# Fixed slots per expert, ranks counted during the attention, and a large-score path at the end: hashed attention with a cosine router on one core

## The chip, the cores and the metric

One core of a Trainium2 chip runs the whole program. The metric is the device time of one execution in microseconds. TensorE (PE) runs matmuls and loads their weights (PEld), VectorE (DVE) and ScalarE (ACT) do elementwise work, GpSimd (POOL) does some elementwise work and issues indirect DMAs, and SyncE (SP) issues the other DMAs. All numbers are 32-bit floats unless bf16 is named.

## The reference, cut to what matters

Attention runs over 4 batches, 8 heads, 768 positions and 64 dimensions. Each query and key gets a bucket from 6 sign bits (its product with `proj`), and a query attends only to keys of its own bucket. The 3072 rows of 512 numbers then go to one of 8 experts each.

```python
q_bits = (np.einsum('bhsd,dk->bhsk', q, proj) > 0)
mask = q_bucket[:, :, :, None] == k_bucket[:, :, None, :]
scores = np.where(mask, scale * np.matmul(q, k.transpose(0, 1, 3, 2)), -1e9)
attn = softmax(scores)
x = (attn @ v).transpose(0, 2, 1, 3).reshape(3072, 512)
logits = normalised(x) @ normalised(expert_emb).T / tau
expert_idx = np.argmax(logits, axis=1)
gate_w = softmax(logits)[np.arange(N), expert_idx]
for e in range(8):
    m = expert_idx == e
    out[m] = gate_w[m, None] * (np.maximum(x[m] @ w1[e], 0) @ w2[e])
```

`w1[e]` is 512 x 1024 and `w2[e]` is 1024 x 512, 2 MB each.

## The kernel before, in words

**Attention.** Work goes by 16 pairs of heads (four per batch). A pair has 12 units (two halves of the queries, six chunks of 128 keys), taken three at a time in four groups. For a group, `scores` makes the products of q and k and of their bucket bits on PE and the exponentials on ACT (L285), and DVE adds them up (L289, L292); `attend` (L300) multiplies the exponentials of the group before with v. Beside the groups stand the steps of the neighbouring pairs. In group 0 these are `prep_features` of q of the next pair (L250 transposes, L251 copies; L246 squares q and k on ACT, for the test of large scores, ahead of the copy) and `sums` (L314) of the pair before. In group 1 they are the same for k, and `finish` (L330, L334, DVE L337 to L348) of the pair before. In group 2 they are `prep_bits` (L263, with DVE L265 for `qb` and L268 for `kb`) and the loads on SP three pairs ahead. The PSUM tiles called `banks` are three buffers of two banks, handed around. `prep_experts` (L195, called at L364) normalises the expert embedding: a load on SP (L197), a square on ACT (L202), a root on POOL, `en` on DVE (L210) and four transposes on PE (L214). It is called before the first scores.

**Routing.** After the last pair of a batch, `route` takes the squares of x on ACT (L133), the best expert and its gate on DVE and POOL, writes the one-hot choice to `oh_all`, and stores the batch with its gates to `xd` in DRAM from SP (L161).

**Between the stages.** If any score could be large, `attention_any` would do the attention again. Every engine reads `beyond_i` and jumps over it (L476). Then PE counts all tokens (L486, L488), DVE makes from this the slot of each token (L490 to L540), 24 small products on PE turn these into a list of token numbers (L546), and `src` (L549) holds it. An expert's tokens fill whole tiles of 128, so 31 tiles always suffice, and 31 are run.

**Experts.** For each tile, `fetch` reads the tile's expert number on SP, loads that expert's `w1` and `w2` (L565, L567, two buffers) and gathers 128 rows from `xd` on POOL (L569). `turn_x` transposes them (L579, copied by L581). The first product has 64 matmuls of 128 columns (L593; a float32 product is two instructions), with a relu on ACT after each half (L596). The second product has 16 matmuls of 512 columns (L601). DVE multiplies by the gate (L603) and POOL scatters the rows (L604). Numbers past the last token are dropped.

The code is issued to each engine in an order that the framework chooses close to the order of the text; each engine then runs its own list in order.

Of the kernel before, what the change touches and what calls it, by code (L numbers as in the profile page):

```python
# [10 lines left out]
U32 = mybir.dt.uint32  # L11
ACT = mybir.ActivationFunctionType
# [3 lines left out]
P = 128  # L16
# [9 lines left out]
def kernel(  # L26
# [26 lines left out]
    NT = (N + E * (P - 1)) // P  # L53
# [31 lines left out]
    iota_t = iota("iota_t", [P, NT], [[1, NT]])  # L85
    iota_n = iota("iota_n", [P, NBLK], [[P, NBLK]])

    tok = iota("tok", [P, B, NC], [[S, B], [1, NC]], base=-N, cm=NC)
# [17 lines left out]
    xh = tc.dram_tile([B * H, S, D], F32, name="xh")  # L106
    half = const.tile([P, NC], F32, name="half")
    nc.vector.memset(half[:], 0.5)
    seg = const.tile([P, E, NBLK], F32, name="seg")
# [12 lines left out]
    oh_all = const.tile([P, E, NBLK], F32, name="oh_all")  # L122
# [3 lines left out]
    BF16 = mybir.dt.bfloat16  # L126


    def route(b, x, l, rp):
        ss = rp.tile([P, NC], F32, name="ss", tag="ss")  # L130
        for c in range(NC):
            sq = rp.tile([P, DM], F32, name="sq", tag="sq")
            nc.scalar.activation(sq[:], x[:, c, 0:DM], ACT.Square, accum_out=ss[:, c : c + 1])  # L133
# [9 lines left out]
        idx = rp.tile([P, NC], F32, name="idx", tag="idx")  # L143
        nc.vector.tensor_reduce(out=idx[:], in_=cand[:], axis=AX.X, op=ALU.min)
        nc.vector.tensor_tensor(
            out=oh_all[:, :, b * NC : (b + 1) * NC].rearrange("p e c -> p c e"),
            in0=iota_e[:].unsqueeze(1).broadcast_to([P, NC, E]),
            in1=idx[:].unsqueeze(2).broadcast_to([P, NC, E]), op=ALU.is_equal,
# [12 lines left out]
        nc.sync.dma_start(xd[b * S : (b + 1) * S, :].rearrange("(p c) w -> p c w", c=NC), x[:])  # L161

# [4 lines left out]
    with ExitStack() as at:  # L167
# [55 lines left out]
        ld, feat, acc, av, zs, xb, lgh = {}, {}, {}, {}, {}, {}, {}  # L223

# [13 lines left out]
        def prep_features(pr, i):  # L238
# [5 lines left out]
            if i == 0:  # L244
                sq = rp.tile([P, 4 * NC * D], F32, name="qksq", tag="qksq", bufs=1)
                nc.scalar.activation(sq[:], qk[:].rearrange("p i c h d -> p (i c h d)"), ACT.Square,  # L246
                                     accum_out=squares[:, pr : pr + 1])
# [3 lines left out]
            nc.scalar.activation(t[:], ps[:, :, 0:SH], ACT.Copy, scale=1.0 if i else DOWN)  # L251

# [69 lines left out]
        def finish(pr):  # L322
# [4 lines left out]
            z, W = zs.pop(pr), P + 2 * E  # L327
            zt = banks()
# [3 lines left out]
            for s in range(2):  # L332
                for c in range(HC):
                    nc.tensor.matmul(ps[:, s, c * W : (c + 1) * W], lhsT=av[pr, s][:, c * P : (c + 1) * P],  # L334
                                     rhs=iden[:, j, :], start=True, stop=True)
            rz = small.tile([P, HC, 4], F32, name="rz", tag="rz")
# [27 lines left out]
        prep_experts()  # L364
        U, PU = len(units), 2 * NC
        for u0 in range(0, U + PU, G):
# [6 lines left out]
            pr, g = u0 // PU, u0 % PU // G  # L373
            if g == 0:
# [3 lines left out]
            elif g == 1:  # L378
                prep_features(pr + 1, 1)
                if pr > 0:  # L380
                    finish(pr - 1)
            elif g == 2:
                prep_bits(pr + 1)
                load(pr + 3)

# [89 lines left out]

    with tc.If(nc.values_load(beyond_i[0:1, 0:1], min_val=0, max_val=1) > 0):  # L476
        attention_any()


    with ExitStack() as so:  # L480
        sp = pool("sp", 1, so)
        ps_o = pool("ps_o", 1, so, space=PSUM)
        flat = "p e n -> p (e n)"

        cnt = ps_o.tile([P, E, NBLK], F32, name="cnt")
        nc.tensor.matmul(cnt[:].rearrange(flat), lhsT=ones[:], rhs=oh_all[:].rearrange(flat), start=True, stop=True)  # L486
        rank = ps_o.tile([P, E, NBLK], F32, name="rank")
        nc.tensor.matmul(rank[:].rearrange(flat), lhsT=tri[:], rhs=oh_all[:].rearrange(flat), start=True, stop=True)  # L488
        upto = sp.tile([P, E, NBLK], F32, name="upto")
        nc.vector.tensor_tensor_scan(out=upto[:].rearrange(flat), data0=seg[:].rearrange(flat),  # L490
                                     data1=cnt[:].rearrange(flat), initial=0.0, op0=ALU.mult, op1=ALU.add)

        full = sp.tile([P, E, NBLK], F32, name="full")
        nc.vector.tensor_tensor(out=full[:], in0=upto[:, :, NBLK - 1 : NBLK].broadcast_to([P, E, NBLK]),  # L494
                                in1=iota_n[:].unsqueeze(1).broadcast_to([P, E, NBLK]), op=ALU.is_gt)
        tiles = sp.tile([P, E], F32, name="tiles")
        nc.vector.reduce_sum(out=tiles[:], in_=full[:], axis=AX.X)
        tend = sp.tile([P, E], F32, name="tend")
        nc.vector.tensor_tensor_scan(out=tend[:], data0=ones[:, 0:E], data1=tiles[:], initial=0.0,
                                     op0=ALU.mult, op1=ALU.add)  # L500

        past = sp.tile([P, NT, E - 1], F32, name="past")
        nc.vector.tensor_tensor(out=past[:], in0=iota_t[:].unsqueeze(2).broadcast_to([P, NT, E - 1]),  # L503
                                in1=tend[:, 0 : E - 1].unsqueeze(1).broadcast_to([P, NT, E - 1]), op=ALU.is_ge)
        texp = sp.tile([P, NT], F32, name="texp")
# [54 lines left out]
    def fetch(t):  # L560
        if t >= NT:
            return
# [74 lines left out]
```

## Time and profile before

| | us |
|---|---|
| median of 3 runs (lowest to highest) | 948.99 (948.25 to 949.33) |
| the profiled execution | 949.78 |
| span of its profile, first to last instruction | 948.1 |
| PE busy | 873.2 (92%) |
| DVE busy | 320.5 (34%) |
| ACT busy | 265.1 (28%) |
| POOL busy | 72.8 (8%) |

The mean granted clock of TensorE is 0.967 of 2.4 GHz. A row of the order of time gives start, duration, engine, line, operation, output and inputs, how many instructions it merges, and in brackets the idle time of the engine before it with what ended it. Matmuls are pipelined: the recorded duration of one is longer than the distance to the next, so distances of starts are the better measure.

### The profile page before, as it was taken

What the parts mean: (1) busy time and instruction counts of PE and PEld (TensorE: products, weight loads), DVE (VectorE), ACT (ScalarE), POOL (GpSimd) and SP (SyncE); (2) the same over time, 40 slices, a digit from 0 to 9 for tenths busy, and PEclk for the clock granted to TensorE, in tenths of its full rate; (3) what the DMA queues carried; (4) which work ended last, traced back from release to release, by engine and by line L of the source; (5) the groups of instructions that cost most, each with busy time, mean ns of one, the idle gap of its engine ahead of it and who ended that gap; (6) DMA issues with size and microseconds to landing.
All of it is one profiled execution on the core that took longest, in us unless ns stands there. A gap on an engine that the chain in (4) does not pass through costs nothing.

```text
span 948.1 us, 12969 instructions
## 1 busy us (share of the span) xinstructions
PE 873.2 (92%) x5397; PEld 538.3 (57%) x5397; DVE 320.5 (34%) x521; ACT 265.1 (28%) x389; POOL 72.8 (8%) x85
## 2 busy tenths in 40 slices
PE   2999999999999999990699999999999999999996
PEld 1444444444444444440576766767677676766764
DVE  4656666666666676655000010101001010000100
ACT  3555555555655554431000100001010000101000
POOL 2000000000000000000101110101111010110100
PEclk8999999999999999995599999999999999999998
DMA  8122223211222210001498889888888888889850
GB/s 196 38 52 50 50 51 118 51 45 39 102 50 50 51 68 1 1 1 69 183 392 307 314 312 325 305 320 313 306 312 313 313 321 312 314 309 323 302 215 1
DMA packets 109121, 170.56 MB, mean 180 GB/s; under 512 B 53302, under 2 KB 57398, under 8 KB 108545
## 3 DMA queue, kind: packets, MB, share of 16 engines
q1 hardware_dynamic: 104064, 155.23, 48.6%
q0 software_dynamic: 4992, 14.44, 3.9%
q8 instruction: 44, 0.72, 0.3%
q14 instruction: 21, 0.16, 0.1%
HBM read 157.06 MB, written 14.43 MB: 181 GB/s over the span
## 4 chain that ended last, share of the span: by engine, by line
issue 27%; DMA 24%; PE 1%; DVE 1%; POOL 0%; POOLq 0%; DVEq 0%
DMA out_dram<-y,src 24%; PE slot L546 1%; DVE row L535 0%; POOL xg L569 0%; POOLq L632 0%; DVE col L538 0%; DVE col L540 0%; DVE pos L521 0%; POOLq L604 0%; DVE upto L490 0%; POOLq L569 0%; DVE past L503 0%; DVE pos_e L519 0%; DVE full L494 0%; DVE pos_e L516 0%
## 5 line engine op out<-in xcount | busy, mean ns | idle before, releaser
L593 PEld LDWEIGHTS ps_h<-xgt,w1t 128*128 128x128 f32 x1984 | 230.1, 193 | 32.4 <-ACT ht L596 18.1
L593 PE MATMUL ps_h<-xgt,w1t 128*128 128x128 f32 x1984 | 236.1, 277 | 10.8 <-ACT ht L596 10.8
L601 PE MATMUL ps_y<-w2t,ht 128*128 128x512 f32 x496 | 218.0, 592 | 0.0
L285 ACT ACTIVATE p<-banks 128x768 f32<-128x768 f32 x192 | 153.5, 810 | 98.0 <-PE banks L282 94.1
L279 PE MATMUL banks<-qt,kt 64*128 64x384 f32 x768 | 165.9, 510 | 3.9 <-ACT p L285 2.4
L596 ACT ACTIVATE ht<-ps_h 128x512 f32<-128x512 f32 x62 | 37.0, 597 | 464.3 <-PE ps_h L593 464.3
L601 PEld LDWEIGHTS ps_y<-w2t,ht 128*128 128x128 f32 x496 | 91.9, 190 | 103.8 <-issue 103.8
L292 DVE TENSOR_TENSOR acc<-acc,p 128x768 f32<-128x768 f32 x128 | 122.7, 958 | 73.9 <-ACT p L285 64.1
L300 PE MATMUL av<-p,vt 128*64 128x385 f32 x768 | 138.1, 495 | 0.0
L603 DVE TENSOR_SCALAR y<-ps_y,xg 128x512 f32<-128x512 f32 x31 | 23.2, 750 | 323.8 <-PE ps_y L601 323.8
L279 PEld LDWEIGHTS banks<-qt,kt 64*128 64x128 f32 x768 | 64.7, 188 | 69.2 <-issue 37.5
L300 PEld LDWEIGHTS av<-p,vt 128*64 128x64 f32 x768 | 49.5, 136 | 76.5 <-issue 76.5
L282 PE MATMUL banks<-qb,kb 64*128 64x384 bf16 x384 | 63.6, 325 | 0.0
L604 POOL DMA_INDIRECT out_dram<-y,src x31 | 31.5, 1015 | 409.4 <-DVE y L603 409.4
L581 DVE COPY xgt<-ps_x 128x512 f32<-128x512 f32 x31 | 21.5, 693 | 111.4 <-PE ps_x L579 101.0
L289 DVE TENSOR_TENSOR acc<-p,p 128x768 f32<-128x768 f32 x32 | 30.6, 957 | 29.9 <-ACT p L285 29.6
L250 PE MATMUL banks<-ident,qk 128*128 128x128 f32 x192 | 29.3, 291 | 8.2 <-DMA qk<-in_q_dram 7.9
L250 PEld LDWEIGHTS banks<-ident,qk 128*128 128x128 f32 x192 | 21.5, 146 | 26.6 <-issue 25.9
L151 POOL TENSOR_TENSOR nrm<-ss,half 128x6 f32<-128x6 f32 x4 | 5.3, 1335 | 403.9 <-ACT sq L133 403.9
L282 PEld LDWEIGHTS <-kb 64*128 64x128 bf16 x384 | 19.5, 95 | 25.3 <-issue 0.9
L569 POOL DMA_INDIRECT xg<-xd,src x31 | 30.3, 977 | 39.4 <-DVE src L549 30.3
L268 DVE TENSOR_SCALAR kb<-banks,ksub 32x768 bf16<-32x768 f32 x32 | 32.5, 1017 | 0.5
(125 smaller groups left out, 395.4 us busy)
## 6 DMA issues: line engine op xcount, KB each, us to landing
w1t<-in_moe_w_dram SPq DMA_DIRECT2D x31, 2048.0 KB, 9.3
w2t<-in_moe_w_dram SPq DMA_DIRECT2D x31, 2048.0 KB, 10.3
xd<-xb SPq DMA_DIRECT2D x4, 1539.0 KB, 6.4
qk<-in_q_dram SPq DMA_DIRECT2D x32, 192.0 KB, 3.8
qk<-in_k_dram SPq DMA_DIRECT2D x32, 192.0 KB, 3.7
vt<-in_v_dram SPq DMA_DIRECT2D x16, 384.0 KB, 3.1
xg<-xd,src POOLq DMA_INDIRECT x31, 7.5
out_dram<-y,src POOLq DMA_INDIRECT x31, 7.6
```

The source lines that it names most:

```text
L250: nc.tensor.transpose(ps[:, c // HC, (c % HC) * P : (c % HC + 1) * P], qk[:, i, c, :, :], ident[:])
L268: nc.vector.tensor_scalar(out=kb[h * D : h * D + 32], in0=ps[h * D + 32 : h * D + 64, :, 0:SH], scalar1=0.0, scalar2=ksub[h * D + 32 : h * ...
L279: nc.tensor.matmul(ps[:, h, 0:SH], lhsT=kt[rows[h], c // HC, kc], rhs=qt[rows[h], s, :], start=True, stop=False)
L282: nc.tensor.matmul(ps[:, h, 0:SH], lhsT=kb[rows[h], c // HC, kc], rhs=qb[rows[h], s, :], start=False, stop=True)
L285: nc.scalar.activation(p[:, :, 0:SH], ps[:, :, 0:SH], ACT.Exp, scale=ESCALE)
L289: nc.vector.tensor_tensor(out=a[:], in0=pts[(u - 1) % NPT][:, :, 0:SH], in1=p[:, :, 0:SH], op=ALU.add)
L292: nc.vector.tensor_tensor(out=a[:], in0=a[:], in1=p[:, :, 0:SH], op=ALU.add)
L300: nc.tensor.matmul(ps[h * D : (h + 1) * D, 0 : SH + 1], lhsT=vt[:, h, c, :], rhs=p[:, h, 0 : SH + 1], start=(c == 0), stop=(c == NC - 1))
L593: nc.tensor.matmul(ps[:, f, :], lhsT=a[:, d, f * P : (f + 1) * P], rhs=xt[:, d, :], start=(d == 0), stop=(d == ND - 1))
L596: nc.scalar.activation(ht[:, f - 3 : f + 1, :], ps[:, f - 3 : f + 1, :], ACT.Relu)
L601: nc.tensor.matmul(py[:], lhsT=ht[:, f, :], rhs=b[:, f, :], start=(f == 0), stop=(f == NF - 1))
L604: nc.gpsimd.indirect_dma_start(out=out[:, :], out_offset=bass.IndirectOffsetOnAxis(ap=src[:, t : t + 1], axis=0), in_=y[:], in_offset=None ...
```

## The change

- **Slots.** Each expert gets three fixed tiles of 128 slots (384 tokens). What is past 384 goes to guarded tiles, of which 25 are written out in nested tests. A tile is run only if the number `nt` of such tiles, worked out on the chip, says so.
- **Ranks per batch.** `count`, `place` and `fill` do the counting, placing and listing for one batch, for batches 0 to 2 inside the attention of the next batch (`count` in `finish` of its pair 0, `place` as a generator from which each group takes four steps, `fill` in `finish` of its pair 1). Batch 3 is placed behind the first expert product. Masks and token numbers are bf16, the numbers in two parts.
- **Early tiles.** Experts 0 and 1 keep their first 256 slots for batches 0 to 2. These four tiles are gathered in the next to last pair and turned before the last `finish`. Their products stand directly behind the attention, and the third tiles of the two experts follow as late tiles.
- **Experts.** A first product takes all tiles of an expert at once (256, 384 or 128 columns), with a relu per 128 hidden rows in one of four PSUM banks. Weights are loaded once per expert, and once per guarded tile that needs others.
- **Large scores.** The jump over `attention_any` is at the end of the program, with an expert stage of its own behind it.
- **Order.** `prep_experts` is called in the fourth group of the first pair. The square of q and k comes behind the copy of k. POOL writes zeros to the last batch's rows of `xd` at the start.

```diff
-    NT = (N + E * (P - 1)) // P
+    KT, EARLY = 3, 2
+    NS = E * KT
+    NO = (N - EARLY * P + EARLY * (2 * P - 2)) // P
...
+    def count(b, cnt, rank):
+        nc.tensor.matmul(cnt, lhsT=ones_b[:], rhs=oh_all[:, b].rearrange("p e c -> p (e c)"), start=True, stop=True)
+        nc.tensor.matmul(rank, lhsT=tri_b[:], rhs=oh_all[:, b].rearrange("p e c -> p (e c)"), start=True, stop=True)
...
+        if b == B - 2:
+            nc.vector.tensor_tensor(out=base[:], in0=upto[:, :, NC - 1], in1=least[:], op=ALU.max)
...
+        yield nc.vector.tensor_tensor(out=rows[:, b], in0=iota_p[:].unsqueeze(1).broadcast_to([P, NC, P]),
+                                      in1=row[:].unsqueeze(2).broadcast_to([P, NC, P]), op=ALU.is_equal)
...
+    def fill(b, ps):
+        col = cols.pop(b)
+        for c in range(NC):
+            nc.tensor.matmul(ps, lhsT=rows[:, b, c], rhs=col[:, c].rearrange("p i t -> p (i t)"),
+                             start=(c == 0), stop=(c == NC - 1))
+        nc.vector.tensor_tensor(out=slots[:], in0=slots[:], in1=ps[:, 0:NS], op=ALU.add)
+        nc.vector.tensor_tensor(out=slots[:], in0=slots[:], in1=ps[:, NS : 2 * NS], op=ALU.add)
...
+    nc.gpsimd.memset(xgs[0][:], 0.0)
+    nc.gpsimd.dma_start(xd[(B - 1) * S : N, :].rearrange("(p c) w -> p c w", c=NC),
+                        xgs[0][:].unsqueeze(1).broadcast_to([P, NC, XW]))
...
-            if i == 0:
-                sq = rp.tile([P, 4 * NC * D], F32, name="qksq", tag="qksq", bufs=1)
...
             nc.scalar.activation(t[:], ps[:, :, 0:SH], ACT.Copy, scale=1.0 if i else DOWN)
+            if i == 1:
+                sq = rp.tile([P, 4 * NC * D], BF16, name="qksq", tag="qksq", bufs=1)
...
-        prep_experts()
...
+            run(4)
...
+            elif g == 3 and pr == 0:
+                prep_experts()
             elif g == 2:
                 prep_bits(pr + 1)
                 load(pr + 3)
+                if pr == 2 * NP:
+                    bring1(0, 0)
+                    bring2(0, 0)
+                if pr == len(pairs) - 2:
+                    early = [[gather(src[0][:, e * KT + i : e * KT + i + 1]) for i in range(2)] for e in range(EARLY)]
+        for e in range(EARLY):
+            ps = banks()
+            for i in range(2):
+                turn_x(xgt[e], i, early[e][i][0], ps[:, i, :])
+        finish(len(pairs) - 1)
...
-    with tc.If(nc.values_load(beyond_i[0:1, 0:1], min_val=0, max_val=1) > 0):
...
+        ps_x, ps_h, ps_y = turns(2, "ps_x"), turns(4, "ps_h"), turns(2, "ps_y")
...
+        def hidden(i, xt, n):
+            for f in range(NF):
+                ph = ps_h()
+                for d in range(ND):
+                    nc.tensor.matmul(ph[:, 0:n], lhsT=w1s[i][:, d, f * P : (f + 1) * P], rhs=xt[:, d, 0:n],
+                                     start=(d == 0), stop=(d == ND - 1))
+                nc.scalar.activation(ht[:, f, 0:n], ph[:, 0:n], ACT.Relu)
...
+        hidden(0, xgt[0], 2 * P)
+        ps = ps_x()
+        count(B - 1, ps[:, 0 : E * NC], ps[:, E * NC : 2 * E * NC])
+        for _ in place(B - 1, ps[:, 0 : 2 * E * NC].rearrange("p (t n) -> p t n", t=2), sp):
+            pass
+        result(0, early[0])
+        fill(B - 1, ps_x()[:, 0 : 2 * NS])
+        late = [tiles_of(e, 2) for e in range(EARLY)]
+        hidden(1, xgt[1], 2 * P)
+        turn(0, late[0])
+        result(1, early[1])
+        nxt = tiles_of(EARLY, 0)
+        hidden(0, xgt[0], P)
...
+        for e in range(EARLY, E):
...
+            hidden(i, xgt[i], KT * P)
...
+            turn(1 - i, nxt)
+            result(i, tiles)
...
+        nt = nc.values_load(ctl[0:1, 2 * NO : 2 * NO + 1], min_val=0, max_val=NO)
+        with ExitStack() as rest:
+            for t in range(NO):
+                rest.enter_context(tc.If(nt > t))
...
+                hidden(i, xgt[i], P)
...
+    with tc.If(nc.values_load(beyond_i[0:1, 0:1], min_val=0, max_val=1) > 0, preferred_fallthrough_block=False):
         attention_any()
...
+        experts_any()
```

## Rows read from the trace of the kernel before

**Rows 1.** Busy time of each engine by stretches, with granted clock and DMA share

```profile
core 0: us, PE busy (x) PEld busy (x) DVE busy (x) ACT busy (x) POOL busy (x), PEclk, DMA share, GB/s
0.00:23.80 23.80, 5.82 (x33) 3.63 (x33) 10.03 (x38) 8.13 (x11) 5.70 (x19) 0.88 0.89 197
23.80:422.20 398.40, 393.11 (x2690) 188.87 (x2693) 250.43 (x375) 215.40 (x302) 4.02 (x3) 0.99 0.18 49
...
433.00:472.80 39.80, 15.09 (x65) 13.81 (x66) 11.35 (x26) 0.00 (x0) 2.96 (x3) 0.50 0.36 137
472.80:939.90 467.10, 456.25 (x2593) 330.14 (x2592) 42.60 (x59) 37.02 (x62) 57.80 (x58) 1.00 0.84 302
939.90:948.10 8.20, 0.07 (x1) 0.00 (x0) 0.75 (x1) 0.00 (x0) 0.98 (x1) 0.70 0.00 0
```

**Rows 2.** Order of time, the start

```profile
9.63 1.28 ACT L246 ACT_TABLE_LOAD   x1 [9.63 <-DMA qk<-in_k_dram]
10.92 1.48 ACT L246 ACTIVATE qksq<-qk 128x1536 f32<-128x1536 f32 x1
...
16.24 0.41 SPq L197 DMA_DIRECT2D emb<-in_moe_expert_emb_dram  x1
...
16.66 2.05 DVE L268 TENSOR_SCALAR kb<-banks,ksub 32x768 bf16<-32x768 f32 x2
...
20.84 0.63 ACT L202 ACTIVATE emb_sq<-emb 8x512 f32<-8x512 f32 x1 [0.27 <-DMA emb<-in_moe_expert_emb_dram]
...
23.30 0.56 PE L214 MATMUL banks<-ident,en 8*128 8x8 f32 x4 [7.77 <-DVE en L210]
...
23.80 1.65 PE L279 MATMUL banks<-qt,kt 64*128 64x384 f32 x4
```

**Rows 3.** Order of time on PE, an expert tile, and the last second product

```profile
497.21 7.03 PE L601 MATMUL ps_y<-w2t,ht 128*128 128x512 f32 x16
...
504.08 3.73 PE L593 MATMUL ps_h<-xgt,w1t 128*128 128x128 f32 x32
...
507.65 0.60 PE L579 MATMUL ps_x<-ident,xg 128*128 128x128 f32 x4
...
508.56 3.84 PE L593 MATMUL ps_h<-xgt,w1t 128*128 128x128 f32 x32 [0.31 <-ACT ht L596]
...
932.94 7.03 PE L601 MATMUL ps_y<-w2t,ht 128*128 128x512 f32 x16
```

**Rows 4.** DMA issues: how many, size, median us from issue to landing

```profile
w2t<-in_moe_w_dram SPq DMA_DIRECT2D x31, 2048.0 KB, 10.3
xd<-xb SPq DMA_DIRECT2D x4, 1539.0 KB, 6.4
...
xg<-xd,src POOLq DMA_INDIRECT x31, 7.5
```

**Rows 5.** Order of time, from the last routing to the first expert product

```profile
433.12 0.34 SPq L161 DMA_DIRECT2D xd<-xb  x1
...
440.13 0.55 DVE L490 TENSOR_TENSOR_SCAN upto<-seg,cnt 128x192 f32<-128x192 f32 x1 [7.04 <-SPq L476]
...
445.82 3.35 DVE L535 TENSOR_TENSOR row<-iota_p,rf 128x3072 f32<-128x3072 f32 x1
...
450.22 10.42 PE L546 MATMUL slot<-col,row 128*128 128x31 f32 x48 [14.32 <-DVE col L540]
...
472.78 5.05 PE L593 MATMUL ps_h<-xgt,w1t 128*128 128x128 f32 x32
```

**Rows 6.** Waits in the attention (us, times, longest), then the end of it in time

```profile
PEld banks L279 <- DVE kb L268: 7.7, 12, 1.1
...
PEld banks L279 <- ACT qksq L246: 5.6, 9, 0.6
...
423.96 1.64 PE L334 MATMUL banks<-iden,o 128*128 128x144 f32 x12
...
426.69 0.23 DVE L348 TENSOR_TENSOR lgh<-banks,rz 128x48 f32<-128x48 f32 x1
```

**Rows 7.** PE's sequencer at the jump, L476: duration min/median/max in ns, start

```profile
L476 PEldq COMPARE_BRANCH  x1: 3532/3532/3532, 428.5 to 428.5; - x1
```

More of the change, by code (lines that the diff above doesn't have):

```diff
@@ L161, in route @@
         nc.sync.dma_start(xd[b * S : (b + 1) * S, :].rearrange("(p c) w -> p c w", c=NC), x[:])
+    base = const.tile([P, E], F32, name="base")
+    nc.vector.memset(base[:], 0.0)
+    least = const.tile([P, E], F32, name="least")
+    nc.vector.memset(least[:], 0.0)
+    nc.vector.memset(least[:, 0:EARLY], 2.0 * P)
+    rows = const.tile([P, B, NC, P], BF16, name="rows")
+    tile_all = const.tile([P, B, NC], F32, name="tile_all")
+    slots = const.tile([P, NS], F32, name="slots")
+    nc.vector.memset(slots[:], 0.0)
@@ new lines, with bring1, bring2 @@
+    NW = 2
+    w1s = [const.tile([P, ND, F], F32, name="w1_0")]
+    w2s = [const.tile([P, NF, DM], F32, name="w2_0")]
+    NX = 6
+    xgs = [const.tile([P, XW], F32, name=f"xg{i}") for i in range(NX)]
+    xgt = [const.tile([P, ND, KT * P], F32, name=f"xgt{i}") for i in range(2)]
+    def bring1(i, e, **kw):
+        nc.sync.dma_start(w1s[i][:], w1[bass.ds(e, 1)].rearrange("o (c p) f -> p (o c) f", p=P), **kw)
+    def bring2(i, e, **kw):
+        nc.sync.dma_start(w2s[i][:], w2[bass.ds(e, 1)].rearrange("o (c p) m -> p (o c) m", p=P), **kw)
@@ L223, with run @@
         ld, feat, acc, av, zs, xb, lgh = {}, {}, {}, {}, {}, {}, {}
+        steps = []
+        def run(n):
+            for _ in range(n):
+                if steps and next(steps[0], None) is None:
+                    steps.pop(0)
         def load(pr):
@@ L327, in finish @@
             z, W = zs.pop(pr), P + 2 * E
+            if j == 1 and b > 0:
+                run(99)
             zt = banks()
@@ L335, in finish @@
                                      rhs=iden[:, j, :], start=True, stop=True)
+            if j == 0 and b > 0:
+                count(b - 1, ps[:, 0, HC * W : HC * W + E * NC], ps[:, 1, HC * W : HC * W + E * NC])
+                steps.append(place(b - 1, ps[:, :, HC * W : HC * W + E * NC], rp))
+                next(steps[0])
+            elif j == 1 and b > 0:
+                fill(b - 1, zt[:, 1, 0 : 2 * NS])
             rz = small.tile([P, HC, 4], F32, name="rz", tag="rz")
@@ L363 @@
         prep_bits(0)
-        prep_experts()
         U, PU = len(units), 2 * NC
-        for u0 in range(0, U + PU, G):
+        early = []
+        for u0 in range(0, U + G, G):
             for u in range(u0, u0 + G):
@@ L573, in turn_x @@
-    def turn_x(t):
-        if t >= NT:
-            return
-        a, b, x = got[t]
-        ps = ps_x.tile([P, DM], F32, name="ps_x", tag="ps_x")
-        for d in range(ND):
-            nc.tensor.transpose(ps[:, d * P : (d + 1) * P], x[:, d * P : (d + 1) * P], ident[:])
-        xt = hp.tile([P, ND, P], F32, name="xgt", tag="xgt")
-        nc.vector.tensor_copy(out=xt[:], in_=ps[:].rearrange("p (d n) -> p d n", n=P))
-        got[t] = a, b, x, xt
-    fetch(0)
-    fetch(1)
-    turn_x(0)
```

365 lines of the change are left out of this document (251 added, 114 removed).

## The prediction

> **What bounds the kernel now.** I read the split of the span into stages first [rows 1]. The attention stretch (23.8 to 422.2) has PE busy for 393 of 398 us at a granted clock of 0.99, with DVE busy for 250 (63%) and ACT for 215. The expert stretch (472.8 to 939.9) has PE busy for 456 of 467 us at 1.00 (2.4 GHz), with the DMA engines at 0.84. Both are PE's, so only PE time removed there counts. Three stretches are not PE's: the start, where the first score matmul stands at 23.80 [rows 2]; the routing gap from 433 to 472.8, with PE busy for 15 of 40 us at 0.50 (1.2 GHz); and a tail of 8.2 us. Then I read the steady expert tile [rows 3]: 16 matmuls of 512 columns start at 497.21 and what follows them at 504.08, so they take 6.87 (0.429 each); half a first product, 32 matmuls of 128 columns, goes from 504.08 to 507.65, 3.57 (0.112 each), and there are two halves; transposes (0.60) and a wait for ACT (0.31) are the rest. From 497.21 to the last second product at 932.94 there are 29 steps of 15.03 us. The program runs 31 tiles because the bound on the number of padded tiles is 31.
>
> **How many tiles there will be.** The inputs have a fixed seed. The reference's own routing gives 464, 461, 375, 317, 367, 377, 373 and 338 tokens. With three fixed tiles per expert that is 24 tiles, and experts 0 and 1 overflow by one each: 26 tiles, five fewer. The first three batches put 337 and 328 tokens on experts 0 and 1, so the 256 early slots are full and cost no extra tile.
>
> **Start.** In the trace the first scores stand behind the four transposes of `prep_experts`, which wait for `en`, which waits for a small load that SP issues only at 16.24 [rows 2]. That is moved behind the third group of the first pair. What is then last is `kb`, done at 16.66 + 2.05 = 18.71. The square of q and k (1.48 + 0.19) no longer stands ahead of the first copy on ACT: 17.0. Against this stands a new transfer: zeros into the last batch's rows of `xd`, 768 rows from POOL, about the 1539 KB whose store takes 6.4 us [rows 4], while the DMA engines are at 0.89 [rows 1]. It can cost nothing or at most the 4.6 us from its issue near 5 to the landing of k at 9.63; the loads of pair 0 were mostly issued before it, so I take 1.3. Scores then start at 18.3, a gain of 5.5 (2.2 to 6.8). On POOL, the memsets of `qb` and `kb` come behind the new memset and this issue; POOL is busy for 5.70 us in this stretch [rows 1] and `kb` is written at 16.66, so several us cover them.
> The Trainium skill (DMA: Bandwidth & Descriptors, section Queues, rings and completion order) says that each DMA engine takes turns between the queues that have work, a packet at a time. By that the loads would run at half speed while the zeros go, the start would gain 2.2 and the sum come out 3.3 us higher; no row of this trace shows both queues busy there.
>
> **Attention.** Three times, PE gets 2 counting and 6 slot matmuls in bf16. The nearest row is L546: 48 instructions of 31 columns in 10.42 us at the lower clock [rows 5], so 0.217 each, about 0.11 at the upper level: 24 x 0.11 = 2.6 us. They have a single pass where the row's have two; none is free on a full PE, so 1.3 to 5.2. `prep_experts` costs its 0.56 of transposes here and a wait of 0 to 2.5 (its chain from 20.84 to 23.30 [rows 2]): I take 1.0 in all, because ACT and DVE have idle time ahead of it. Moving the square behind the copy of k gives back part of the 5.6 us for which weight loads wait on it, mostly on ACT standing at a load [rows 6]: 2.5 (0 to 5.6). Placing a batch is about 22 DVE instructions, mostly on a quarter of the elements of L490's 0.55 us [rows 5], one row test a quarter as wide as L535 (0.84), and the adds of the slots: about 6 us per batch, spread four steps to a group. A pair takes 24.9 us, of which DVE uses 15.7, so the idle 9 hide it; without that cover it would be 18 us in all. SP gets 4 MB of weights at the ninth pair, when DMA is at 0.18 [rows 1]; POOL gets four gathers that wait for the slots of batches 0 to 2, with 25 us before their use. Sum: +1.1.
>
> **From attention to the first expert product.** The last matmuls of `finish` (L334) end at 425.60 [rows 6]. Ahead of them stand 4 x 4 transposes, 0.60 each four [rows 3]: 2.4. The PSUM banks are read until 426.92 by L348, so another 1.0 (0 to 1.3). The first expert product starts at 429.0 - 5.5 + 1.1 = 424.6, in place of 472.78 [rows 5]. What was between is hidden: the routing of batch 3 (425.6 to 433.1), its store, the jump, the placing (440.1 to 460.6), the gather and the first weights. On ACT the relus come behind the squares and an exponential of this routing; four `ps_h` banks hold the first 4 x 1.7 us of products, which is just enough.
>
> **Expert stage.** The rows give 0.112 at 128 columns and 0.429 at 512; a straight line gives 0.217 at 256 and 0.323 at 384, and three pieces of 128 would bound the last from above at 0.335 (+5 us in all). First product: six experts x 64 x 0.323 = 124, two early ones of 256 columns 27.8, two late and two overflow tiles 4 x 7.14 = 28.6. Second product: 26 x 6.87 = 178.6. Transposes: 22 tiles x 0.60 = 13.2, and 0.5 at each of six turns of three tiles, which have two banks: 3. Last count and slots 0.9. Sum 376.1, or 14.5 us per tile. Weights fall from 31 to 10 loads of 4 MB; each has 20 us or more of cover where it now lands in 10 [rows 4].
> The late tiles' chain: store of `xd` issued at 433.1 + 2.4 - 4.4 = 431, landed by 438; slots ready behind the second product of expert 0, at 424.6 + 13.9 + 13.7 + 1 = 453; gather 1.1 + 7.5 [rows 4], and two scatters ahead on POOL at 1.3: 464, needed at 467. It holds by 3 us.
>
> **Branches and tail.** The jump over the large-score code goes from its present place to the end, and the two overflow tiles stand in nested tests. One jump is in the trace: PE's compare took 3.53 us [rows 7]. PE's two taken bodies follow the test directly, and queued matmuls cover them, so I take 1.0 for both (0 to 7.1). The exits cost PE nothing that anyone waits for; at the very end SP has to pass two exits after the last scatter: 1.5 (0 to 4). The tail is otherwise the same 8.2.
> The Trainium skill (Runtime: NRT & Kernel Launch, section Instruction fetch mechanics) states that a taken branch to code outside the fetched window stalls for a fetch, which speaks against putting tests into the expert stage; PE's 3.53 us agrees, and by it alone at each of three tests the sum would be 9.6 higher, the second rival below.
>
> **Sum.** 424.6 + 376.1 + 1.0 + 8.2 + 1.5 = 811.3 of span. The profiled execution is 949.78 for a span of 948.1, so 1.7 lies around it: 813.0. The median shown, 948.99, is 0.8 lower: 812.2.
>
> **Rivals.**
> 1. DVE doesn't hide the placing: PE waits for 18 us over three batches: 830. For it: DVE feeds `kb` and the accumulators, and weight loads already wait 7.7 us on `kb` [rows 6]. Against: 9 us idle in each pair. Chance 0.13.
> 2. Every test costs PE the 3.53: two bodies and the last exit, with the 1.0 replaced: 822. For: [rows 7]. Against: in that row PE had nothing queued. Chance 0.12.
> 3. The late tiles come 5 to 10 us late, because the slack of 3 us is used up by POOL or the store: 820, a little more with the clock. Chance 0.09.
> 4. The early tiles don't do what they are for: the first product waits until the store of `xd` lands (439.5 now), through a buffer taken over from the attention. PE idles for 14 us and restarts at 1.2 GHz for some 5 us of work, as the 5.07 against 3.57 of the first half tile shows [rows 3, 5]: 830. Chance 0.07.
> 5. Slower than before: the expert stage runs at 1.2 GHz. Each us of its work then costs one more; the 137 us gained are gone once 137 of the 376 do so, and all of it gives 1188. For: the clock was at 0.50 over the gap. Against: over 467 us it was 1.00 with a wait such as the 0.31 us in every tile [rows 1, 3], and the new order has fewer. Chance 0.02.
>
> **How the numbers follow.** The sum has 0.56. I predict 812.2. The low ends of start (-1.3), attention (-4), banks (-1), turns (-3) and tests with tail (-2.5) give 801; rivals 1 to 4 reach 830, and with the upper ends of the start (3.3) and of the straight line (4.6) 838. 801 to 838 leaves out rival 5 and mixes. About 0.2% is what a measurement of this kernel can tell from no change; only rival 5 and things unseen lie there: faster 0.97, same 0.01, slower 0.02.
>
> **What the new profile would show.** First score matmul near 18; the square behind the copy of k; the attention's last L334 near 424 and first expert product near 425; clock 1.00 throughout; 384-column matmuls 0.32 us apart; 26 scatters; PE's last product near 802. Wrong if PE idles over 3 us anywhere behind the attention, if pairs 5, 9 and 13 (counted from 0) are longer than others, or if more than two guarded tiles run.

## The result, and the profile after

The changed kernel takes 824.65 us (median of four runs, 823.36 to 826.12) against 949.16 (948.25 to 950.64) for the kernel before: ratio 0.8687, 95% interval 0.8669 to 0.8706. 812.2 was predicted, with a range of 801 to 838. The profiled execution took 824.79 for a span of 822.7, where the sum had 811.3: the sum is 11.4 short. Every part below is counted in spans.

Busy time by stretches, the same view as [rows 1] (clock, DMA share and GB/s at the end of a line):

```profile
core 0: us, PE busy (x) PEld busy (x) DVE busy (x) ACT busy (x) POOL busy (x), PEclk, DMA share, GB/s
0.00:23.80 23.80, 4.20 (x19) 3.02 (x23) 7.99 (x41) 4.64 (x6) 6.67 (x21) 1.00 0.97 172
23.80:422.00 398.20, 388.84 (x2684) 186.47 (x2678) 262.85 (x448) 215.52 (x305) 8.64 (x8) 1.00 0.25 67
422.00:450.00 28.00, 26.56 (x155) 19.16 (x152) 12.18 (x35) 9.34 (x25) 1.34 (x1) 1.00 0.53 207
...
500.00:800.00 300.00, 297.78 (x994) 165.00 (x993) 29.62 (x44) 29.13 (x68) 37.60 (x38) 0.99 0.41 144
800.00:822.70 22.70, 9.97 (x44) 5.79 (x43) 1.44 (x2) 1.11 (x4) 1.00 (x1) 0.81 0.09 23
```

The gap of [rows 1], 40 us at 0.50 with PE busy for 15, is gone: from 422 to 450 PE is busy for 26.56 of 28 at 1.00. DMA's share in the expert stretch is 0.41, where it was 0.84. But the first 23.8 us have PE busy for 4.20 (5.82 before), and DVE's busy time in the attention rose by 12.4.

The start, in order of time, to be read beside [rows 2]:

```profile
4.27 0.95 POOL L270 DMA_DIRECT2D xd<-xg  x1
...
8.99 8.30 SPq L363 DMA_DIRECT2D qk<-in_k_dram  x1
...
17.95 2.79 PE L376 MATMUL banks<-ident,qk 128*128 128x128 f32 x12 [17.95 <-DMA qk<-in_q_dram]
...
20.06 1.48 ACT L380 ACTIVATE qksq<-qk 128x1536 bf16<-128x1536 f32 x1
...
21.55 0.79 ACT L377 ACTIVATE qt<-banks 128x768 f32<-128x768 f32 x1
...
29.38 2.22 ACT L415 ACTIVATE p<-banks 128x768 f32<-128x768 f32 x3 [4.39 <-PE banks L412]
```

POOL issues the zeros at 4.27. SP then stands for 8.30 us at one load of k, and the first transposes wait for q until 17.95; they stood at 7.90 before. The first exponential is at 29.38 (before: 25.81). It was to come 5.5 earlier and comes 3.6 later. The square still runs ahead of the copy of q: the order of the text was changed, but not the order in which the framework issued it, and this holds for every pair (below).

PE, in order of time, from the attention's last value product to the end (x is a count; the second column runs to the end of the group):

```profile
425.33 4.10 PE L430 MATMUL av<-p,vt 128*64 128x385 f32 x24
...
435.83 14.08 PE L692 MATMUL ps_h<-xgt,w 128*128 128x256 f32 x64 [1.42 <-DVE beyond L543]
...
521.62 20.80 PE L692 MATMUL ps_h<-xgt,w 128*128 128x384 f32 x64
542.26 1.04 PE L284 MATMUL ps_x<-ident,xg 128*128 128x128 f32 x8
...
776.77 7.31 PE L692 MATMUL ps_h<-xgt,w 128*128 128x128 f32 x64
786.30 0.90 PE L284 MATMUL ps_x<-ident,xg 128*128 128x128 f32 x4 [2.22 <-DMA xg<-xd,osrc]
787.00 8.52 PE L700 MATMUL ps_y<-w,ht 128*128 128x512 f32 x16
...
802.93 7.03 PE L700 MATMUL ps_y<-w,ht 128*128 128x512 f32 x16
```

The first expert product (435.83) stands 6.4 us behind the last value product, where it was 50.6. A first product of 384 columns takes 542.26 - 521.62 = 20.64, or 0.3225 for each of 64; 0.323 was forecast. (The end of a last product is taken as its start and 16 x 0.429, the distance of starts.) All but one of the turns stand without a wait: the second guarded tile waits 2.22 us for its gather, and the 16 matmuls behind that wait take 8.52 instead of 7.03. The last product ends at 809.8, so the tail is 12.9 us, against 8.2 before [rows 1].

Against the terms of the sum: start 9.1 too low, attention 2.5 too low (first exponential to last value product 400.05, before 396.4, where 1.1 more was forecast), gap 0.4 too high, expert stage 3.1 too high (374.0 for 377.1 with the tests, the late gather included), tail 3.2 too low (12.9 for 9.7). That is the 11.4. Theory: the zeros cost the start, the late gather and the way out of the tests cost the end, and the other terms are off by less.

### The profile page after: what moved, and what is told of

It is laid out like the page before. It is cut to its first block, busy times and chain, and to the rows that moved or that the text cites. A ratio compares the mean times of both kernels' runs of the same rounds, so it can differ in the third digit from the quotient of the medians.

```text
span 822.7 us, 10275 instructions
## 1 busy us (share of the span) xinstructions
PE 777.3 (94%) x4089; PEld 412.1 (50%) x4089; DVE 327.5 (40%) x618; ACT 265.4 (32%) x423; POOL 65.6 (8%) x79
## 5 line engine op out<-in xcount | busy, mean ns | idle before, releaser
L692 PE MATMUL ps_h<-xgt,w 128*128 128x384 f32 (+2 forms) x768 | 182.3, 398 | 1.4 <-DVE beyond L543 1.4
L700 PE MATMUL ps_y<-w,ht 128*128 128x512 f32 x416 | 183.1, 596 | 0.0
L692 PEld LDWEIGHTS ps_h<-xgt,w 128*128 128x128 f32 x768 | 126.2, 191 | 58.5 <-issue 4.3
L694 ACT ACTIVATE ht<-ps_h 128x384 f32<-128x384 f32 (+2 forms) x96 | 38.5, 402 | 323.9 <-PE ps_h L692 319.2
L700 PEld LDWEIGHTS ps_y<-w,ht 128*128 128x128 f32 x416 | 78.3, 192 | 91.8 <-issue 91.8
L285 DVE COPY xgt<-ps_x 128x512 f32<-128x512 f32 x23 | 15.3, 689 | 168.2 <-PE ps_x L284 168.2
L704 DVE TENSOR_SCALAR y<-ps_y,xg 128x512 f32<-128x512 f32 x26 | 19.5, 751 | 147.7 <-PE ps_y L700 147.7
L705 POOL DMA_INDIRECT out_dram<-y,src x24 | 24.6, 1024 | 287.4 <-DVE y L704 273.0
L393 PE MATMUL banks<-qt,proj 128*32 128x384 f32 x128 | 25.7, 512 | 3.1 <-ACT qt L377 1.7
```

The lines of the kernel that those rows point to most:

```text
L393: nc.tensor.matmul(ps[r0 : r0 + 32, s, 0:SH], lhsT=proj2[:, h, :], rhs=feat[pr, i][:, s, :], start=True, stop=True)
L692: nc.tensor.matmul(ph[:, 0:n], lhsT=w1s[i][:, d, f * P : (f + 1) * P], rhs=xt[:, d, 0:n], start=(d == 0), stop=(d == ND - 1))
L694: nc.scalar.activation(ht[:, f, 0:n], ph[:, 0:n], ACT.Relu)
L700: nc.tensor.matmul(py[:], lhsT=ht[:, f, j * P : (j + 1) * P], rhs=w2s[i][:, f, :], start=(f == 0), stop=(f == NF - 1))
```

## The experiments

Each is set against the changed kernel unless its expectation says otherwise; all shared runs of the kernel before, whose medians lay between 948.87 and 949.43.

**The zeros, later.** The transfer is issued by SP at the end of the first batch's routing, with that batch's rows; any finite numbers serve there.

```diff
-    nc.gpsimd.dma_start(xd[(B - 1) * S : N, :].rearrange("(p c) w -> p c w", c=NC),
-                        xgs[0][:].unsqueeze(1).broadcast_to([P, NC, XW]))
...
+        if b == 0:
+            nc.sync.dma_start(xd[(B - 1) * S : N, :].rearrange("(p c) w -> p c w", c=NC), x[:])
```

> The zeros for the last batch's rows of `xd` are no longer sent at the start; instead the first batch's rows are stored there a second time, at about 140 us. Theory (the zeros hold up the loads of the first pair): first transposes back from 17.95 to 8 to 10, first exponential near 20 in place of 29.4, total about 815 (812 to 818). Rival (the start is late for a reason of SP's own queue, the zeros only stand beside it): unchanged, 823 to 826.

813.36 us (811.14 to 813.88), 11.3 less. The first transposes are back at 7.92 and the first exponential is at 20.65. So without the zeros the start gains 5.2 against the kernel before: the forecast's 5.5, less 0.3. By the rows the zeros' price is 9.9: the first expert product stands at 425.98 for 435.83. The other 1.6 of the 11.4 in spans arise in the expert stage, where the 16 matmuls behind the guarded gather's wait take 7.03 for 8.52; nothing shows that to be the zeros' doing. The queues show how the transfer took it. First the changed kernel's, 8 to 12 us (packets, MB, share of the 16 engines; q1 is SP's queue with the loads, q0 POOL's with the zeros):

```profile
DMA packets 208, 0.46 MB, mean 114 GB/s; under 512 B 103, under 2 KB 103, under 8 KB 208
...
q0 software_dynamic: 105, 0.43, 105.4%
q1 hardware_dynamic: 103, 0.03, 16.1%
```

Then this kernel's in the same stretch:

```profile
DMA packets 2957, 1.07 MB, mean 266 GB/s; under 512 B 2702, under 2 KB 2957, under 8 KB 2957
...
q1 hardware_dynamic: 2957, 1.07, 115.7%
```

While both queues had work they moved 105 and 103 packets: one for one. But a packet of the zeros holds 4.1 KB (0.43 MB / 105) and one of the loads 0.3 KB, so the loads got 0.03 MB where they get 1.07 alone. The Trainium skill (DMA: Bandwidth & Descriptors, section Queues, rings and completion order) has engines take turns between queues packet by packet, and this trace agrees with 105 to 103. The prediction read it as half the speed for the loads; turns of unequal packets left them 3% of their bytes in this stretch.

**The zeros on SP's own queue**, behind the five loads of pair 0.

```diff
-    nc.gpsimd.dma_start(xd[(B - 1) * S : N, :].rearrange("(p c) w -> p c w", c=NC),
-                        xgs[0][:].unsqueeze(1).broadcast_to([P, NC, XW]))
...
         for pr in range(3):
             load(pr)
+            if pr == 0:
+                nc.sync.dma_start(xd[(B - 1) * S : N, :].rearrange("(p c) w -> p c w", c=NC),
+                                  xgs[0][:].unsqueeze(1).broadcast_to([P, NC, XW]))
```

> The same zeros with the same pieces of 2052 bytes, but issued by SP behind the loads of the first pair, so that one queue carries everything. Theory A (it is the second queue that takes turns with the loads): the first pair's loads land as in the kernel before, total 813 to 818. Theory B (any 1.5 MB that early costs the same, because later loads of q and k come late instead): 821 to 826.

818.19 us (815.48 to 820.39), between the two. The first transposes are at 8.01 and the first exponential at 20.95, so pair 0 loses nothing. This run changes two things, the queue and the place behind the five loads, and no run splits them. But the loads of the next pairs stand behind the zeros (SP is at one load of k for 4.40 us from 11.35 and at one of v for 4.22 from 15.79), and the first sums come at 48.64, where they come at 45.90 in the run above, the first expert product at 428.33 for 425.98. So of the 9.9 us, 2.4 stay when the same bytes stand behind the loads. Of the 4.8 between the medians of the two runs, 1.7 are again the matmuls behind the gather's wait (8.73 here for 7.03).

**The gather of the next guarded tile, one test ahead.**

```diff
                 nxt = [gather(osrc[:, 0:1])]
+                ahead = [gather(osrc[:, 1:2])]
...
-                if t + 1 < NO:
-                    nxt = [gather(osrc[:, t + 1 : t + 2])]
+                nxt = ahead
+                if t + 2 < NO:
+                    ahead = [gather(osrc[:, t + 2 : t + 3])]
```

> The second guarded tile's rows are gathered before the first test, one tile further ahead. Theory (PE waits 2.2 us at 784 for this gather and then runs its next matmuls slower by 1.5): 3.7 less, 821.0. Rival (that gap is the test itself, which comes at the same place): 824.7, with the wait under another name.

818.66 us (818.29 to 820.28): 6.0 less in the medians, 4.6 in the spans. PE in order of time, the same turn and second product as above:

```profile
776.17 7.31 PE L692 MATMUL ps_h<-xgt,w 128*128 128x128 f32 x64
783.31 0.60 PE L284 MATMUL ps_x<-ident,xg 128*128 128x128 f32 x4
783.75 7.03 PE L700 MATMUL ps_y<-w,ht 128*128 128x512 f32 x16
```

No wait, and 7.03 for the 16 matmuls. In the changed kernel the 1.5 behind the wait came at a granted clock of 0.91 from 784 to 803. By the first and the last product the stage takes 369.8 here (435.22 to 805.07) for 374.0: the gather cost 4.1. A start that was 0.6 earlier makes up the 4.6, and the medians' extra 1.4 has no row.

**No tests.** This kernel leaves out the guarded tiles past the second and the large-score path.

```diff
-        nt = nc.values_load(ctl[0:1, 2 * NO : 2 * NO + 1], min_val=0, max_val=NO)
...
-            for t in range(NO):
-                rest.enter_context(tc.If(nt > t))
+            for t in range(2):
...
-    with tc.If(nc.values_load(beyond_i[0:1, 0:1], min_val=0, max_val=1) > 0, preferred_fallthrough_block=False):
-        attention_any()
-        experts_any()
```

> The two guarded tiles run without tests; guarded tiles past the second and the large-score path are left out. Theory (leaving the nested tests and the last one takes POOL through increments of its DMA semaphores and a second drain, 4.7 us more tail): tail from 12.9 back to 8 to 9 and total 820 to 821, with PE's time per tile unchanged. Rival A (tests cost PE itself, up to 3.5 each): 813 to 817. Rival B (the tail is the scatter's): 824.7.

813.81 us (812.52 to 814.16), 7 below what was expected: without a test POOL issues the second gather early (736.85), so the gain of the run above is in it too. The sum of both lies where the rival put a test's cost on PE (813 to 817), but PE's stage refutes it: first to last product take 369.8 us here (435.04 to 804.88), without tests, and 369.8 in the run above, with them. PE's last product ends at 804.88, 4.9 sooner, and the tail is 7.6, 5.3 shorter. What filled the tail shows in POOL's sequencer (duration min/median/max in ns, then first and last start). In the changed kernel:

```profile
L829 POOLq INC_SWDGE_SEM  x1: 1288/1288/1288, 814.7 to 814.7; - x1
...
L847 POOLq TENSOR_LOAD <-beyond_i x1: 313/313/313, 816.2 to 816.2; - x1
...
L875 POOLq DRAIN  x3: 50/113/4658, 817.2 to 822.4; - x3
```

and here:

```profile
L870 POOLq DRAIN  x3: 40/107/5787, 805.9 to 812.2; - x3
```

The last drain takes some 5 us in both. Here it begins at 805.9, right where POOL turns to the last scatter; there it begins at 817.2, 5.2 us behind the end of the last scatter's issue (812.03), after POOL has left the nested tests (816.1) and passed the last jump (L847). 4.1 of the 5.2 stand ahead of the last jump; this run leaves out both, so it does not price them apart. PE's own branches at the tests, in the changed kernel:

```profile
L829 PEldq COMPARE_BRANCH  x4: 65/146/3557, 769.9 to 810.2; - x4
```

The ones on the way in take 0.07 to 0.10 us; one of 3.56 lies on the way out, behind PE's last product. The Trainium skill (Runtime: NRT & Kernel Launch, section Instruction fetch mechanics) ties such a stall to taken branches. This trace agrees, and the tests into whose bodies PE falls cost it nothing: its products are contiguous from 776.17 in the run above, and the stage is as long as without tests. Rival 2 falls.

**Narrow first products**, each in pieces of 128 columns.

```diff
-                for d in range(ND):
-                    nc.tensor.matmul(ph[:, 0:n], lhsT=w1s[i][:, d, f * P : (f + 1) * P], rhs=xt[:, d, 0:n],
+                for j in range(n // P):
+                    js = slice(j * P, (j + 1) * P)
+                    for d in range(ND):
+                        nc.tensor.matmul(ph[:, js], lhsT=w1s[i][:, d, f * P : (f + 1) * P], rhs=xt[:, d, js],
```

> The change with each 384-column instruction of the first product split into three of 128 columns, all else kept. Theory: an instruction costs its columns plus a small fixed part: three of 128 at 0.112 us are 0.336 in place of 0.3225; with 64 such sets in each of 26 tiles (1,664 sets x 0.0135) that is +22 us at most if every set is split, so 845 to 848 against 824.65. Rival: the wider instruction buys nothing because the weight loads, or the transfer of the weights, set the pace of the stage: then within 2 us of 825.

827.79 us (826.93 to 830.29): 3.1 more. The expectation counted the sets wrong: only six experts have three tiles in one product, so 6 x 64 sets, which at 0.0135 make 5.2. PE, the product that took 20.64 above:

```profile
521.00 21.60 PE L694 MATMUL ps_h<-xgt,w 128*128 128x128 f32 x192
542.43 1.04 PE L284 MATMUL ps_x<-ident,xg 128*128 128x128 f32 x8
```

It takes 21.43, so 0.79 for each of six experts, and the two early products take 0.48 each more: 5.7 by the rows. In spans the run is 2.4 longer: its stage began 1.6 us earlier, and the matmuls behind the gather's wait took 7.03, 1.5 less, which is nearly all of the difference. So the columns matter, but all of the widening is worth under 6 us.

**The kernel before with 26 tiles.**

```diff
-    NT = (N + E * (P - 1)) // P
+    NT = 26
```

> The kernel before with 26 expert tiles in place of 31, all else kept. Theory: its stage is paced by TensorE at 15.03 us a tile, so five tiles fewer are 75 us: 873 to 875 against 949.16. Then 75 of the 124.5 us that the change gained are tiles, and some 50 are the gap after the attention, the narrower instructions and the rest. Rival: the 4 MB of weights of each tile pace the stage of before (DMA share 0.84): then a tile fewer still takes its own time off, but the tiles that are left run unchanged and the remaining 50 us would be those of the repeated weights.

872.43 us (871.48 to 873.27): 76.7 less for five tiles, 15.3 each. So of 124.5 us, 77 are tiles that hold no token, and 48 are all the rest. In spans (870.8 to 822.7) those 48 are: the expert stage 392.1 to 374.0, 18.1 gained; last value product to first expert product 49.7 to 6.4, 43.3 gained; the end of the attention 7.9 later; the tail 5.4 longer.

**No early tiles.** Counting, placing and listing of the last batch first, then gathers, turns and the first product.

```diff
-                if pr == len(pairs) - 2:
-                    early = [[gather(src[0][:, e * KT + i : e * KT + i + 1]) for i in range(2)] for e in range(EARLY)]
...
+        fill(B - 1, ps_x()[:, 0 : 2 * NS])
+        early = [[gather(src[1][:, e * KT + i : e * KT + i + 1]) for i in range(2)] for e in range(EARLY)]
+        turn(0, early[0])
+        hidden(0, xgt[0], 2 * P)
+        turn(1, early[1])
...
```

> The change without the early expert tiles: the same counting, placing and filling for the last batch, but the first gathers, their turns and the first product only behind them. Theory: TensorE then stands from the last value product (429.4 us) until the last slot is stored, gathered and turned, as in the kernel before: the first product comes at about 454 in place of 435.8, and a few us of the stage run at the lower clock: +18 to +22, 843 to 847. Rival: the early tiles hide only the placing, and the rest is short: +10, 835.

842.85 us (842.66 to 844.86): 18.2 more. PE in order of time:

```profile
443.36 0.40 PE L246 MATMUL ps_x<-col,rows 128*128 128x48 bf16 x6 [7.86 <-DVE col L239]
450.75 1.12 PE L284 MATMUL ps_x<-ident,xg 128*128 128x128 f32 x4 [7.00 <-DMA xg<-xd,src]
...
454.45 15.96 PE L686 MATMUL ps_h<-xgt,w 128*128 128x256 f32 x64
```

The first product stands at 454.45, 18.6 later, and takes 15.96 where it took 14.08. From the last value product it is 26.1 us, between the 6.4 of the change and the 49.7 of the run above. So of the 43.3 us by which this gap shrank, 19.7 are the early tiles'. The other 23.6 come with the placing of three batches inside the attention and the smaller steps that are left; no run splits these two.

**The preparation of the experts, back ahead of the first scores.** Against the run with the zeros later.

```diff
+        prep_experts()
...
-            elif g == 3 and pr == 0:
-                prep_experts()
```

> The change with the zeros' transfer moved behind the first loads (as in e1_zeros_later, 813.36), and with the preparation of the expert constants moved back ahead of the first scores. Theory: moving the preparation behind the first scores is worth 4 to 5 us at the start: 817 to 818. Rival: the first scores wait for the loads and the square root whatever is issued beside them: within 1 us of 813.4.

820.47 us (820.11 to 821.48): 7.1 more in the medians and 8.0 in the spans, above the 4 to 5. PE waits 6.79 for `en`, and the granted clock falls (PE in order of time, then two stretches):

```profile
22.73 0.56 PE L337 MATMUL banks<-ident,en 8*128 8x8 f32 x4 [6.79 <-DVE en L333]
```

```profile
20.00:24.00 4.00, 1.27 (x6) 1.00 (x8) 1.60 (x9) 0.99 (x4) 0.58 (x1) 0.50 1.17 269
24.00:28.00 4.00, 4.00 (x18) 1.78 (x14) 0.78 (x5) 2.77 (x4) 0.00 (x0) 0.50 1.00 384
```

The first exponential comes 4.6 later (25.23); the other 1.4 of the 6.0 by which the first sums come late (51.9 for 45.9) arise in pair 0, whose first stretch runs at 0.50, where the run it is set against has 1.00 throughout. The first expert product is still 6.0 late (431.97 for 425.98). The last 2 us are not the preparation's: 1.7 of them are the 16 matmuls behind the guarded gather, 8.73 here for 7.03.

**Both gains at once**: the zeros later and the gather ahead, by the two edits above.

> Two edits together on the change: the zeros' transfer behind the first loads (e1_zeros_later, 813.36) and the guarded gathers issued one test ahead (e3_gather_ahead, 818.66 against 824.65). Theory: one sits at the start and the other at the end of the expert stage, so they add: 813.36 less 4.6 (by the spans) to 6.0 (by the medians), 807.4 to 808.8. Rival: they share a cause, the transfers, and the sum comes short: 811 to 813.

810.40 us (810.16 to 810.80), 3.0 below the zeros alone and 14.3 below the change: ratio 0.8541 (0.8529 to 0.8553). It falls 1.6 short of the expected range and just outside the rival's, and not for the rival's reason: in the run with the zeros alone the wait for the gather is 2.31 and the 16 matmuls behind it take 7.03. The slow 8.52 after the wait was not there to be gained. The runs with the wait differ in this: 8.09 to 8.73 behind it in five kernels, 7.03 in three, at waits of 2.22 to 2.46 and 2.03 to 2.31. The granted clock goes with it: 0.83 from 786 to 796 in the change and 0.81 from 779 to 788 with the zeros on SP, but 1.00 from 777 to 784 in the run with the zeros later. What decides it stays open.

**The square, back ahead of the copy.** Against the run with the zeros later.

```diff
             feat[pr, i] = t
+            if i == 0:
+                sq = rp.tile([P, 4 * NC * D], BF16, name="qksq", tag="qksq", bufs=1)
+                nc.scalar.activation(sq[:], qk[:].rearrange("p i c h d -> p (i c h d)"), ACT.Square,
+                                     accum_out=squares[:, pr : pr + 1])
```

> The kernel of e1_zeros_later (813.36) with the square of q and k put back ahead of the first copy, in bf16 as in the change. Theory: the move of the square is worth nothing, because the ordinary pairs take 24.85 us before and after: within 1 us of 813.36. Rival, as forecast: it gives back 2.5 us of PE's waits, and undoing it costs as much: 815.9.

813.08 us (812.78 to 814.29): nothing. But the edit moved nothing either: on every engine this run's trace has the same instructions in the same order as that of the run it is set against. The framework places the square where it did before, whatever the order of the text. So this is that kernel measured once more, and no test of the move. From the first sums to the last it takes 373.4 us, the other run 373.6.

**All of a batch's placing at once.** Against the same run.

```diff
-            run(4)
+            run(99)
```

> The kernel of e1_zeros_later (813.36) with all of a batch's placing issued at once, at the second group of the pair, in place of four steps to a group. Theory: DVE's idle time hides the placing because it is spread; some 6 us in one piece stand ahead of what PE needs from DVE and cost 1 to 4 us in each of three batches: 816 to 825. Rival: 9 idle us in a pair of 25 hide it in any order: within 1 us of 813.4.

812.32 us (811.99 to 814.52): 1.1 below the run it is set against, with the ranges of the two overlapping. But this edit moved nothing either: the order on every engine is the same in both, and in both a batch's placing, from its scan to its last product, already stands in one piece with a single other instruction between (DVE there, then here):

```profile
156.97 0.26 DVE L208 TENSOR_TENSOR_SCAN upto<-seg,first 128x48 f32<-128x48 f32 x1
...
161.60 0.53 DVE L241 TENSOR_TENSOR col<-hit,tok 128x144 bf16<-128x144 f32 x2
```

```profile
156.32 0.26 DVE L208 TENSOR_TENSOR_SCAN upto<-seg,first 128x48 f32<-128x48 f32 x1
...
160.95 0.53 DVE L241 TENSOR_TENSOR col<-hit,tok 128x144 bf16<-128x144 f32 x2
```

The four steps to a group never reached the engine, so no run here compares a spread placing with one in a piece. My theory of 1 to 4 us for a piece falls all the same: the pair in which it stands is 0.3 us longer than an ordinary one (25.14 for 24.85, from sums to sums), its two counting matmuls included.

**The small loads of the projection behind the five of pair 0**, on top of both gains.

```diff
-    for h in range(2):
-        for r in range(2):
-            nc.sync.dma_start(proj2[h * D : (h + 1) * D, h, r * NB : (r + 1) * NB], proj[:, :])
...
             load(pr)
+            if pr == 0:
+                for h in range(2):
+                    for r in range(2):
+                        nc.sync.dma_start(proj2[h * D : (h + 1) * D, h, r * NB : (r + 1) * NB], proj[:, :])
```

> The kernel of e9_both with the four small loads of proj (2.57 us of SP's issue time, from 2.21 us on) moved behind the five loads of pair 0. Theory: the second halves of pair 0's q and k are issued 2.6 us earlier, the first transposes come at 5.5 to 6 in place of 7.92, and the kernel is 1.5 to 2.5 us shorter than e9_both: 805.5 to 806.5 if that takes 808. Rival: the loads are limited by their bytes (DMA share 0.97 at the start), or the projection then waits for its constants: within 0.5 us of e9_both, or slower.

809.93 us (809.51 to 811.60), the same as with both gains alone, as the rival has it; my 805.5 to 806.5 was wrong. The transposes do come earlier (6.39 for 8.05) and the first exponential 3.9 earlier (16.38 for 20.29), but the first sums only 0.8 (44.75 for 45.54). PE's waits between, and a stretch of this kernel:

```profile
PE banks L405 <- DVE iden L340: 2.0, 1, 2.0
```

```profile
32.00:45.00 13.00, 10.98 (x62) 4.70 (x66) 9.20 (x18) 3.88 (x6) 0.00 (x0) 0.87 0.66 246
```

The moved preparation of the experts is late next: PE waits 2.0 for its copies to `iden` (0.7 with both gains alone), and the clock is 0.87 in that stretch (1.00 with both gains alone).

## Why the prediction was right, and where it failed

**The sign and the size** came from three terms, and all held. The tiles: 26 instead of 31, 77 us by the run that changes only their number. The gap: 6.4 us from the last value product to the first expert product where 6.8 were forecast. The wide product: 0.3225 against 0.323 from a straight line between 128 and 512 columns. The clock was 1.00 from 435.8 to 784 and 0.91 from there to 803, so rival 5 had nothing to stand on. (Of the range, the low ends as named add up to 11.8, which gives 800.4 and not 801.)

**The step that failed is the zeros' price**, "nothing or at most the 4.6 us from its issue near 5 to the landing of k", of which 1.3 was taken. It cost 9.9, by the first expert product with and without it. "The loads of pair 0 were mostly issued before it" was not so: at 4.27 two of the five were, and the next two followed at 4.81 and 5.45. Nor would it have been enough, since a load that is issued has still to land, and POOL's 4.1 KB packets took turns with its small ones. The bound itself was wrong. It let the zeros delay the loads only until the time at which k used to land, and not by as long as the zeros themselves needed: 38.7% of the first 24 us in the changed kernel's queue view, which is 9.3 us of all 16 engines, for a store priced at 6.4 [rows 4]:

```profile
q0 software_dynamic: 432, 1.58, 38.7%
```

The rest of the start held: 5.2 without the zeros for 5.5, and the moved preparation is what brings it (6.0, with the clock).

**The attention** was short by 2.5, all of it the square: "2.5 (0 to 5.6)" given back was 0. The step that failed comes ahead of its price: the edit did not move the square. From the third copy of q on, ACT runs squares, copies and exponentials in the same order before and after, and five squares have run by then, so that each stands some two pairs ahead of the copies of its own pair. ACT before, then after:

```profile
107.99 0.81 ACT L251 ACTIVATE kt<-banks 128x768 f32<-128x768 f32 x1 [2.08 <-PE banks L250]
...
113.79 1.48 ACT L246 ACTIVATE qksq<-qk 128x1536 f32<-128x1536 f32 x1 [1.32 <-DMA qk<-in_k_dram]
...
126.53 0.81 ACT L251 ACTIVATE qt<-banks 128x768 f32<-128x768 f32 x1 [2.08 <-PE banks L250]
```

```profile
111.87 0.81 ACT L377 ACTIVATE kt<-banks 128x768 f32<-128x768 f32 x1 [2.08 <-PE banks L376]
...
117.68 1.48 ACT L380 ACTIVATE qksq<-qk 128x1536 bf16<-128x1536 f32 x1 [1.32 <-DMA qk<-in_k_dram]
...
130.41 0.81 ACT L377 ACTIVATE qt<-banks 128x768 f32<-128x768 f32 x1 [2.08 <-PE banks L376]
```

Nor do the rows show that a move would have paid. The 5.6 of [rows 6] are waits of PEld. PE's own waits before, from 52 to 422 us, are these three, and none names the square:

```profile
PE banks L279 <- ACT p L285: 2.2, 2, 1.1
PE banks L263 <- ACT p L285: 1.4, 3, 0.5
PE banks L279 <- DVE kb L268: 0.4, 1, 0.4
```

What a real move would be worth no run shows. Ordinary pairs take 24.85 before and after. A batch's counting, placing and listing makes the two pairs in which they stand 0.9 to 1.0 longer together, 3.0 in all for a forecast of 2.6. These lengths refute rival 1, which had 6 us a batch.

**The expert stage** was too high by 3.1 in spite of the gather. With the gather ahead the stage is 369.8, 7.3 below the forecast. A turn of four transposes takes 0.44 from start to start (783.31 to 783.75 in the run with the gather ahead) in place of the 0.60 that was taken from the end of a row: 3.5 over 22 tiles. The 3.0 for turns of three tiles and the 1.0 for the tests were not spent.

**The tail** was given 1.5 (0 to 4) for the exits and took 4.7, because POOL's sequencer, not SP's, is last through them and drains only then (817.17; SP's last compare at L847 is at 814.35). **The guarded gather** was in no term: the sum asked whether a test costs PE, and not which issue a test holds back. POOL could issue the second guarded tile's rows only behind the first test, at 779.38, 4.7 us before PE wanted them. It is rival 3's mechanism at another place; the late tiles themselves, with the slack of 3 us, were on time.

Of the signs named at the end of the prediction, the first scores near 18 and the last product near 802 were wrong by the zeros and the gather, "the square behind the copy of k" was wrong in every pair, and pairs 5, 9 and 13 are longer, though by 0.2 to 0.3 us (the pair behind each by 0.75) and not by 6.

## What to carry to other kernels

Price a transfer on another queue by the time in which it holds the engines and by the size of its packets against those it competes with, not by whether the rival loads were issued first; here 4.1 KB packets left those of 0.3 KB 3% of their bytes. When work goes inside a test, ask for each queue which issue can no longer run ahead of it, and which engine is last out. Before a wait of the weight loader is counted as a gain, look for it among PE's own waits. And look in the trace whether an edit of the text moved an instruction at all: two of the edits here did not, and their equal times say nothing about the order.

## What was not expected of the hardware

Two queues with work took turns by packets (105 and 103 in 4 us), so that 1.5 MB from POOL reduced the loads' bytes in that stretch to 3%. Together they moved 114 GB/s at a DMA share of 1.21, where the loads alone moved 266 at 1.16. Leaving the nested tests and passing the last jump kept POOL for 5.2 us ahead of its last drain. And a wait of 2.0 to 2.5 us on PE was followed by 16 slower matmuls (8.09 to 8.73 us) in five kernels and by none (7.03) in three, with no clear border in its length.
